# Sparse attention feeding an ELU MLP on one core: the opening and the first chunk in another order, and the second batch's masks added to its scores on TensorE

## The chip, the core and the metric

The kernel runs on one core of a Trainium2 chip. A core has five engines that each take their instructions in order: PE (TensorE, matrix multiplies, with the weight loads shown apart as PEld), DVE (VectorE), ACT (ScalarE), POOL (GpSimd) and SP (SyncE). They wait for each other through semaphores. Matrix products land in PSUM, in banks of 512 float32 columns; everything else lies in SBUF. Transfers between DRAM and SBUF are issued by POOL and SP and run on 16 DMA engines.

The metric is the device time of one execution in microseconds (us). Before the change the median of three runs is 324.32 us (323.88 to 326.67).

## The reference

Attention over 8 batches, 8 heads, 576 positions and 64 dimensions is followed by a two-layer MLP:

```python
scores = scale * np.matmul(q, k.transpose(0, 1, 3, 2))       # 8 x 8 x 576 x 576
rel = pos[:, None] - pos[None, :]
mask_local = (rel >= 0) & (rel < 32)                         # heads 0 to 3
mask_strided = (rel >= 0) & (pos[None, :] % 32 == pos[:, None] % 32)   # heads 4 to 7
scores = np.where(masks, scores, -1e9)
attn = softmax(scores)
x = (attn @ v) as 4608 tokens x 512
h = x @ w_in                                                 # 512 -> 2048
g = np.where(h > 0, h, np.exp(np.minimum(h, 0)) - 1)         # ELU
out = g @ w_out                                              # 2048 -> 512
```

A local head needs the keys of the last 32 positions; a strided head the earlier positions with the same remainder by 32, at most 18 of them. Most of the 576 x 576 scores are never computed.

## The kernel before, in words

**Attention.** A batch is worked as four pairs of heads: two strided ones (s0, s1 in batch 0, S0, S1 in batch 1) and two local ones (l0, l1). Keys and queries are brought into 126 or 108 rows (strided: seven or six residues of 18 positions) or blocks of 96 queries against 128 keys (local), so that all wanted scores lie in small blocks with a fixed mask. The steps of a pair are: `t_q` and `t_k`, transposes on PE into a PSUM bank and a copy to SBUF; `s0` and `s1`, score matmuls into the two banks of `pair_a` (L500), the exp on ACT into a probability tile `pr` (L508) and for every batch but 0 at once the mask, a multiplication of `pr` by 0 and 1 on DVE (L523; batch 0 has it as steps `m0`, `m1`); `a0` and `a1`, probabilities times values (L542), whose extra column of ones gives the sums of the softmax, then a reciprocal and a multiplication on DVE (L550, L551) into `x_s` or `x_l`; and `x`, the transposes of that (L578, L591) and the copies into `xT` (L585, L587, L595). `halo` copies 32 rows of the local values into the place where the next block of 96 reads them (L428). The strided values are loaded as `v_raw` and reordered into `v_str` by two copies (L421). From batch 3 on the transposes of q and k are made by DMAs and the steps are grouped otherwise; the change does not touch that.

**MLP.** Nine chunks of 512 tokens. `moe_in` (four matmuls of 128x512, L629) computes 128 of the 2,048 hidden units into a PSUM bank, `moe_act` takes the ELU: an exp on ACT (L655), a min and subtraction on DVE (L662), a maximum with the bank on DVE (L664). In chunk 0 the hidden blocks 4, 7, 10, 13 and 15 have a Relu on ACT (L658) and one DVE instruction (L659) in place of the last two. `moe_out` (four matmuls, L678) is one part of the second product; after four parts the result is copied by ACT (L683) and sent off by SP.

**Order.** There is no scheduler: the program order on each engine is the order in which the Python code emits. The opening (batch 0, and the first part of chunk 0) follows the list `OPENING`. In it `fill.n` are n matmuls of 128x512 whose result nobody reads, into a bank not used yet, and `moe.c` is the part of the first three blocks of chunk 0 that needs the feature group c (0 and 1 local, 2 and 3 strided) of `xT`. Then every chunk nb runs 16 steps s; batch nb + 1's attention pieces are put into gaps: gap 2s ahead of `moe_in(s)`, gap 2s + 1 behind `moe_act(s)`, then `moe_out` parts of the chunk before (for chunk 0 its own, given by `outs`). Which gap a piece takes is start + pitch x pair + offset, from `TIMES`. `ON_VECTOR` names the steps of batch 0 whose copy is made by DVE; the others are made by ACT.

**Buffers.** Scores use `pair_a` alone after the opening, so a pair's next scores wait for the exp of the last. Transposes, `av` results and `x` transposes go through a ring of three PSUM banks (`singles[:3]`): each use waits until the one three uses earlier was read. `moe_in` has the two `half` banks and, in the first part of chunk 0, `singles[3]`, which `moe_out` takes over when `share` is called at s = 10.

**Loads.** POOL issues nearly all of them. At most eight are under way: each issue waits for the one eight back. Behind the loads of batch 0 stand w_in(0), q and k and v of batch 1 with w_in(1) among them, w_in(2), w_in(3), four parts of w_out, and batch 2.

## Time and profile before

| | |
|---|---|
| median of three runs | 324.32 us (323.88 to 326.67) |
| the profiled execution | 324.63 us |
| its span, first to last instruction | 322.7 us |
| mean granted PE clock | 0.993 of full speed |
| opening, to the end of `moe.1` | 27.3 us |
| chunk 0, to the first matmul of chunk 1 | 27.3 to 55.8 us |
| last matmul | 318.2 us |

The page's second part cuts the span into 40 slices of 8.07 us; a digit is the busy share in tenths, and PEclk the clock that PE was granted. A row of the waits reads: engine, tile and line that waited, what released it, microseconds in total, times, longest. A row of the stretches gives the stretch in us, its length, then busy time and (instructions) of PE, PEld, DVE, ACT and POOL, the granted clock, the DMA share and GB/s. A row of the timeline gives start, duration, engine, line, operation, tile written<-tiles read, shapes and, in brackets, the idle time ahead of it with what ended it.

### The profile page before, as it was taken

The numbers are of one execution on the slowest core, as the hardware profiler recorded it, in microseconds if no ns is written. First come the engines' busy times: TensorE is split into PE (matmuls) and PEld (weight loads), VectorE is DVE, ScalarE is ACT, GpSimd is POOL, SyncE is SP. The second block draws the span as 40 slices with busy tenths as digits, with TensorE's granted clock in tenths as the row PEclk, the third lists the DMA queues.
The fourth block names the chain that finished last, engine by engine and source line by source line (L and its number), as shares of the span: only waits on it lengthen the run. The fifth ranks groups of instructions, "written<-read, shape, count | busy, mean of one in ns | idle before, by whom it ended". The sixth has DMA issues, their size and how long they took to land.

```text
span 322.7 us, 6076 instructions
## 1 busy us (share of the span) xinstructions
PE 304.5 (94%) x2214; PEld 151.6 (47%) x2214; DVE 244.9 (76%) x539; ACT 175.9 (55%) x334; POOL 140.1 (43%) x218
## 2 busy tenths in 40 slices
PE   1997988999999999999999999999999999999994
PEld 0564444555544544444444444444444444444443
DVE  6576887787888988989798879887988566776610
ACT  3668885776555554555555565565555534434411
POOL 9859725958957839978942840000000000000000
PEclk9999899999999999999999999999999999999999
DMA  6999999999999999999994994291110000010012
GB/s 108 159 174 121 168 207 138 145 134 174 90 149 176 141 141 186 77 159 168 196 134 102 125 208 95 71 152 58 54 51 34 35 32 35 37 62 34 35 67 72
DMA packets 108970, 36.33 MB, mean 113 GB/s; under 512 B 87357, under 2 KB 104453, under 8 KB 108933
## 3 DMA queue, kind: packets, MB, share of 16 engines
q0 software_dynamic: 71632, 18.10, 62.4%
q1 hardware_dynamic: 37301, 17.77, 26.9%
q8 instruction: 19, 0.31, 0.4%
q14 instruction: 18, 0.15, 0.1%
HBM read 36.70 MB, written 9.44 MB: 143 GB/s over the span
## 4 chain that ended last, share of the span: by engine, by line
PE 85%; DVE 6%; ACT 3%; DMA 2%; issue 1%; POOL 1%; ACTq 0%; POOLq 0%
PE single L678 37%; PE half L629 27%; PE single L629 9%; PE single L542 3%; PE pair_a L463 2%; ACT e_sb L655 2%; PE single L382 2%; DMA k_str<-in_k_dram 2%; DVE g_sb L664 1%; DVE x_l L551 1%; PE single L578 1%; DVE e_sb L662 1%; PE single L368 1%; PE pair_a L500 1%; PE single L724 1%
## 5 line engine op out<-in xcount | busy, mean ns | idle before, releaser
L678 PE MATMUL single<-w_out_sb,g_sb 128*128 128x512 bf16 (+1 forms) x592 | 145.9, 373 | 0.0
L629 PE MATMUL half<-xT,w_in_sb 128*128 128x512 bf16 x436 | 113.4, 382 | 0.0
L655 ACT ACTIVATE e_sb<-half 128x512 f32<-128x512 f32 x109 | 65.3, 599 | 69.7 <-PE half L629 67.4
L662 DVE TENSOR_SCALAR e_sb<-e_sb 128x512 bf16<-128x512 f32 x139 | 64.0, 460 | 36.0 <-ACT e_sb L655 34.9
L678 PEld LDWEIGHTS <-g_sb 128*128 128x128 bf16 x592 | 55.2, 98 | 57.6 <-DVE g_sb L664 0.2
L629 PEld LDWEIGHTS <-w_in_sb 128*128 128x128 bf16 x576 | 52.0, 98 | 56.7 <-issue 2.2
L664 DVE TENSOR_TENSOR g_sb<-e_sb,half 128x512 bf16<-128x512 bf16 x104 | 71.5, 688 | 3.7
L629 PE MATMUL single<-xT,w_in_sb 128*128 128x512 bf16 x140 | 36.5, 379 | 0.0
L655 ACT ACTIVATE e_sb<-single 128x512 f32<-128x512 f32 x35 | 21.0, 600 | 24.2 <-PE single L629 22.0
L683 ACT COPY o_sb<-single 128x512 f32<-128x512 f32 (+1 forms) x37 | 21.3, 576 | 17.0 <-PE single L678 16.7
L542 PEld LDWEIGHTS <-pr 128*128 128x128 bf16 (+3 forms) x352 | 21.0, 106 | 15.6 <-issue 0.9
L469 ACT ACTIVATE pr<-pair_a 126x936 bf16<-126x936 f32 (+1 forms) x20 | 19.2, 962 | 12.5 <-PE single L463 12.5
L180 POOL DMA_DIRECT2D k_str<-in_k_dram x32 | 20.7, 662 | 10.7 <-DMA w_in_sb<-in_moe_w_in_dram 3.0
L664 DVE TENSOR_TENSOR g_sb<-e_sb,single 128x512 bf16<-128x512 bf16 x35 | 24.1, 688 | 1.2
L180 POOL DMA_DIRECT2D v_raw<-in_v_dram x32 | 19.9, 648 | 9.4 <-DVE v_str L421 7.5
L180 POOL DMA_DIRECT2D q_str<-in_q_dram x28 | 17.6, 650 | 6.4 <-DMA w_in_sb<-in_moe_w_in_dram 1.9
L551 DVE TENSOR_TENSOR x_l<-single,rden 96x384 bf16<-96x384 f32 x32 | 17.7, 553 | 1.1
L551 DVE TENSOR_TENSOR x_s<-single,rden 126x256 bf16<-126x256 f32 (+1 forms) x32 | 15.7, 491 | 1.1
L203 POOL DMA_DIRECT2D q_loc<-in_q_dram x20 | 15.5, 817 | 2.3 <-PE single L382 0.8
L203 POOL DMA_DIRECT2D k_loc<-in_k_dram x20 | 15.8, 820 | 0.7 <-DMA q_loc<-in_q_dram 0.5
L508 ACT ACTIVATE pr<-pair_a 128x576 bf16<-128x576 f32 (+2 forms) x20 | 13.0, 652 | 5.6 <-PE pair_a L500 5.5
L550 DVE RECIPROCAL rden<-single 96x6 f32<-96x6 f32 (+2 forms) x64 | 11.9, 185 | 3.3 <-PE single L542 2.7
(114 smaller groups left out, 261.6 us busy)
## 6 DMA issues: line engine op xcount, KB each, us to landing
out_dram<-o_sb SPq DMA_DIRECT2D x35, 256.0 KB, 3.1
v_loc<-in_v_dram POOLq DMA_DIRECT2D x8, 288.0 KB, 7.9
k_str<-in_k_dram POOLq DMA_DIRECT2D x32, 67.5 KB, 5.0
v_raw<-in_v_dram POOLq DMA_DIRECT2D x32, 67.5 KB, 4.7
w_in_sb<-in_moe_w_in_dram POOLq DMA_DIRECT2D x4, 512.0 KB, 10.0
w_out_sb<-in_moe_w_out_dram POOLq DMA_DIRECT2D x4, 512.0 KB, 16.5
q_str<-in_q_dram POOLq DMA_DIRECT2D x28, 67.5 KB, 7.2
q_loc<-in_q_dram POOLq DMA_DIRECT2D x20, 64.0 KB, 4.4
```

The lines of the kernel that those rows point to most:

```text
L180: engine.dma_start(out=t[0:108, h].rearrange("p g d -> p (g d)"), in_=rows[h, :, 0:30, :].rearrange("t (r g) d -> t r (g d)", g=5))
L203: nc.gpsimd.dma_start(out=t[:, h // 2, 0:4, h % 2], in_=src[name][b, h, 0:512].rearrange("(i p) d -> p i d", p=128))
L469: nc.scalar.activation(both, sc[0:nk, :, 0:w], ACT.Exp, scale=scale)
L508: nc.scalar.activation(halves, sc[0:nk, :, 0:w], ACT.Exp, scale=scale)
L542: nc.tensor.matmul(av[0:m, p, blk - b0, :], lhsT=pr[0:nk, o:o + m], rhs=vt[0:nk, 2 * self.hp + p, blk, :], start=True, stop=True)
L551: nc.vector.tensor_tensor(self.x[0:nq, b0:b0 + n].rearrange("q g p d -> q p g d"), av[0:nq, :, 0:n, 0:D], r.unsqueeze(3).to_broadcast([nq, ...
L629: nc.tensor.matmul(hps, lhsT=w_in_sb[:, c, m * 128:(m + 1) * 128], rhs=xT[:, c, nb * N_TILE:(nb + 1) * N_TILE], start=start, stop=stop)
L655: nc.scalar.activation(e_sb, hps, ACT.Exp)
L662: nc.vector.tensor_scalar(e1_sb, e_sb, scalar1=1.0, scalar2=1.0, op0=ALU.min, op1=ALU.subtract)
L664: nc.vector.tensor_tensor(g_of[nb][:, m, :], e1_sb, hps, op=ALU.max)
L678: nc.tensor.matmul(ops, lhsT=g_of[nb][:, m, kk * 128:(kk + 1) * 128], rhs=w_out_sb[:, m, cols], start=(m == 0), stop=(m == MC - 1))
L683: nc.scalar.copy(o_sb, ops)
```

## The change

It has these parts:

1. `OPENING` puts s1.halo ahead of l1.s1, l0.a0 between s1.x and s0.x, l0.x ahead of moe.3, and S0.t_q behind moe.3; two of the eight `fill` matmuls are left out.
2. Batch 1's pieces in chunk 0 no longer come from `TIMES` but from a list `SECOND` with a gap for each. S0.t_k moves from gap 1 to 3, S0's scores from gaps 3 and 5 to 5 and 7, S1's first scores come at gap 9, the halo from gap 13 to 21 (behind `moe_act(10)`), l0.a0 from gap 19 (behind `moe_act`) to 22.
3. Batch 1's masks leave DVE. Two tiles are made in the opening, `far_s` and `far_l`, 0 where a score is wanted and -1e30 elsewhere. Ahead of the score matmuls two matmuls with the identity as weights write them into the two banks (start), and the scores are added to them (start=False); the exp then gives 0 where the mask was 0.
4. Batch 1's v_str copies go from ACT to POOL, in POOL's queue between the load of v_loc and that of w_in(3); w_in(2) is now loaded ahead of v_loc of batch 1. S1.t_q's copy goes from ACT to DVE.
5. Batch 2 starts at gap 5 of chunk 1 instead of 4. Chunk 0's three `moe_out` parts come at steps 12, 14 and 15 instead of 11, 13 and 15, and `share` is called at s = 11.

The order on PE from the end of the opening, as the two programs emit it (S0.s0+ are the far matmuls and the scores):

```
before  t_k S0 | s0 S0 | s1 S0 | moe 3 | a0 S0 | t_k S1 | moe 4 | a1 S0 | s0 S1 | moe 5 | s1 S1 | x S0 | t_q l0 | moe 6 ...
after   t_k S0 | s0+ S0 | moe 3 | s1+ S0 | t_k S1 | moe 4 | s0+ S1 | moe 5 | a0 S0 | s1+ S1 | a1 S0 | moe 6 | a0 S1 | t_q l0
        | moe 7 | a1 S1 | x S0 | t_k l0 | moe 8 | t_q l1 | x S1 | s0+ l0 | moe 9 | t_k l1 | s1+ l0 | moe 10 | s0+ l1 | a0 l0
        | moe 11 | a1 l0 | s1+ l1 | moe 12 | out | a0 l1 | x l0 | moe 13 | a1 l1 | moe 14 | out | x l1 | moe 15 | out
```

The diff, cut to its core:

```diff
 PIECES = (-2, -1, 0, 2, 3, 5, 7, 0)
 TIMES = (
     None,
-    (3, 6, (-3, -2, 0, 2, 4, 6, 9, 3)),
-    (4, 6, (-3, -2, 0, 2, 4, 6, 8, 0)),
+    None,
+    (5, 6, (-3, -2, 0, 2, 4, 6, 8, 0)),
     (2, 7, PIECES),
     ((2, 8, 15, 22), 0, PIECES),
 )
...
+SECOND = """
+3 S0.t_k 5 S0.s0 7 S0.s1 8 S1.t_k 9 S1.s0 11 S0.a0 11 S1.s1 12 S0.a1 13 S1.a0 14 l0.t_q
+15 S1.a1 15 S0.x 16 l0.t_k 17 l1.t_q 18 S1.x 18 l0.s0 19 l1.t_k 20 l0.s1 21 S1.halo 21 l1.s0
+22 l0.a0 24 l0.a1 24 l1.s1 26 l1.a0 26 l0.x 27 l1.a1 30 l1.x
+""".split()
 OPENING = """
 s0.cast_q s0.t_q s0.t_k s1.cast_q s1.t_k s0.s0 s0.m0 s1.t_q s0.s1 s0.m1 fill.2 l0.t_q s1.s1
 s1.m1 s1.s0 s1.m0 l0.t_k l1.t_q fill.1 s0.v l0.s0 l0.m0 l1.t_k l0.s1 s1.a0 s0.a0 l0.m1 l1.s0
-s1.a1 s0.a1 fill.1 l1.s1 l1.m0 fill.1 s1.halo s1.x fill.1 s0.x l1.m1 fill.1 l0.a0 fill.1 l0.a1
-l1.a0 moe.2 l1.a1 S0.t_q l0.x S1.t_q moe.3 l1.x moe.0 moe.1
+s1.a1 s0.a1 s1.halo fill.1 l1.s1 l1.m0 fill.1 s1.x l0.a0 l1.m1 fill.1 s0.x l0.a1 l1.a0 moe.2
+l1.a1 l0.x moe.3 S0.t_q l1.x S1.t_q moe.0 moe.1
 """.split()
-ON_VECTOR = "s0.t_q s1.cast_q s1.t_k l0.t_q s0.v l1.x".split()
+ON_VECTOR = "s0.t_q s1.cast_q s1.t_k l0.t_q s0.v l1.x S1.t_q".split()
 ON_SCALAR = (4, 7, 10, 13, 15)
...
     identity = consts.tile([128, 128], BF16, tag="identity")
     mask_l = consts.tile([128, S], BF16, tag="mask_l")
     mask_w = consts.tile([128, 2 * 126 + 3 * 108], BF16, tag="mask_w")
+    far_l = consts.tile([128, 3 * LB], BF16, tag="far_l")
+    far_s = consts.tile([128, 126], BF16, tag="far_s")
     mask_s, mask_s3 = mask_w[:, 0:252], mask_w[:, 252:576]
     rden = consts.tile([128, B, 2, 2, 2, 6], F32, tag="rden")
     ones = consts.tile([128, 1], BF16, tag="ones")
...
     BY_DMA = 3
     WHOLE = 3
+    FAR = 1
     raw = {}
     src = {"q": q, "k": k, "v": v}
...
     clear_v(0)
     nc.vector.memset(kT["loc"][0][:, :, 0:32], 0.0)
+    nc.vector.tensor_scalar(far_s[0:126], mask_s[0:126, 0:126], scalar1=1.0,
+                            scalar2=-NEG, op0=ALU.subtract, op1=ALU.mult)
+    nc.vector.tensor_scalar(far_l, mask_l[:, 0:3 * LB], scalar1=1.0, scalar2=-NEG,
+                            op0=ALU.subtract, op1=ALU.mult)
     load_strided(0, "k")
     load_local(0, "q")
     load_local(0, "k")
...
     load_strided(1, "v")
     load_local(1, "q")
     load_local(1, "k")
+    load_w_in(2)
     load_local(1, "v")
-    load_w_in(2)
+    for o, i in zip(rows_of(v_str[1][:, :, :, 0:D], slice(0, 4)),
+                    rows_of(raw[1], slice(0, 4))):
+        nc.gpsimd.tensor_copy(o, i)
     class Pair:
...
         def copy(self, step, late):
-            if self.b == 0:
-                late = f"{self.name}.{step}" in ON_VECTOR
+            if self.b < 2:
+                name = self.name.upper() if self.b else self.name
+                late = f"{name}.{step}" in ON_VECTOR
             return nc.vector.tensor_copy if late else nc.scalar.copy
         def cast(self, name):
...
                 return
             sc = rings["sc"].next()
             blocks = self.blocks(u)
+            far = self.b == FAR
+            if far:
+                k, n = blocks[0][4:]
+                g = len(blocks) // 2
+                if self.strided:
+                    t = far_s[0:k, 0:n].unsqueeze(1).to_broadcast([k, g, n])
+                elif u == 0:
+                    t = far_l
+                else:
+                    t = far_l[:, n:2 * n].unsqueeze(1).to_broadcast([k, g, n])
+                for bank in range(2):
+                    nc.tensor.matmul(sc[:, bank, 0:g * n], lhsT=identity[0:k, :],
+                                     rhs=t, start=True, stop=False)
             for p, blk, bank, i, nk, nq in blocks:
                 at, half = self.place(p, blk)
                 d = slice(64 * half, 64 * half + 64)
...
                 nc.tensor.matmul(sc[:, bank, i * nq:(i + 1) * nq],
                                  lhsT=kT[kind][self.b % 2][d, at, c:c + 128],
                                  rhs=qT[kind][self.b % 2][d, at, c:c + nq],
-                                 start=True, stop=True)
+                                 start=not far,
+                                 stop=not far or i == len(blocks) // 2 - 1)
             nk, nq = blocks[0][4:]
             w = len(blocks) // 2 * nq
             pr = (p_p if self.b else p_p0).tile([128, 1152 if self.b else 648], BF16, tag="pr", name="pr")
             halves = pr[0:nk, 0:2 * w].rearrange("k (a x) -> k a x", a=2)
             nc.scalar.activation(halves, sc[0:nk, :, 0:w], ACT.Exp, scale=scale)
             self.pr[u] = pr
-            if self.b:
+            if self.b and not far:
                 self.mask(u)
         def mask(self, u):
...
                         identity[0:LB, 0:LB])
                 self.copy("x", self.b > 1)(dst, xt[:, 0:S])
+    def second():
+        pairs.update((f"l{hp}", Pair(1, False, hp)) for hp in range(2))
+        gaps = {}
+        for gap, step in zip(SECOND[::2], SECOND[1::2]):
+            pair, what = step.split(".")
+            gaps.setdefault(int(gap), []).append(
+                lambda p=pairs[pair], what=what: p.step(what))
+        return gaps
     def attention(b, start, pitch, at):
         gaps = {}
         pairs = [Pair(b, s, hp) for s in (b < LATE, b >= LATE) for hp in range(2)]
...
         if b >= LATE:
             gaps[begin[0]] = [pairs[3].halo]
         for i, pr in enumerate(pairs):
-            if b == 1 and pr.strided:
-                pr.t_q = lambda: None
             for off, piece in ((at[0], pr.t_q), (at[1], pr.t_k),
                                (at[7], lambda pr=pr: pr.v_in(0)),
                                (at[7] + (b > 1), lambda pr=pr: pr.v_in(1)),
...
     def outs(nb, s):
         if nb == 0:
-            return [(0, i) for i in range(3) if s == 11 + 2 * i]
+            return [(0, i) for i in range(3) if s == (12, 14, 15)[i]]
         step = [(nb - 1, i) for i in range(3, MC)]
         if nb < n_chunks:
             step += [(nb, i) for i in range(3)]
...
     for nb in range(n_chunks + 1):
         if nb + 1 < B:
-            gaps = attention(nb + 1, *TIMES[min(nb + 1, 4)])
+            gaps = attention(nb + 1, *TIMES[min(nb + 1, 4)]) if nb else second()
             if nb == 0:
                 share([pair_a], b_halves + singles[3:], [], singles[:3])
             elif nb + 1 < LATE:
...
         if nb + 3 < B:
             load_batch(nb + 3)
         for s in range(MC):
-            if nb == 0 and s == 10:
+            if nb == 0 and s == 11:
                 share([pair_a], b_halves, singles[3:], singles[:3])
             if s == (9 if nb + 2 > LATE else 6) and nb > 0 and nb + 2 < B:
                 transpose_batch(nb + 2, int(nb + 2 >= LATE))
```

## The prediction

> **What bounds the kernel now.** I read the page first (busy shares, slices), then what TensorE (PE) waited for, then busy time and clock in short stretches, then PE's timeline against those of ScalarE (ACT) and VectorE (DVE).
>
> ```profile
> PE 304.5 (94%) x2214; PEld 151.6 (47%) x2214; DVE 244.9 (76%) x539; ACT 175.9 (55%) x334; POOL 140.1 (43%) x218
> PE   1997988999999999999999999999999999999994
> PEclk9999899999999999999999999999999999999999
> ```
>
> PE is the bound from the third slice on; only the first 56 us leave it gaps. The waits of PE name them:
>
> ```profile
> PE pair_a L500 <- ACT pr L508: 1.3, 3, 0.7
> PE single L578 <- DVE x_s L551: 1.1, 2, 0.7
> PE pair_a L500 <- ACT kT_str L371: 0.8, 1, 0.8
> PE single L542 <- ACT v_str L421: 0.5, 1, 0.5
> ```
>
> Between the opening's last fused part (end 27.31) and the first matmul of chunk 1 (55.76) the timeline shows eight waits of PE, 4.5 us together. The stretches show a second loss:
>
> ```profile
> 28.00:32.00 4.00, 2.31 (x23) 1.46 (x24) 3.81 (x7) 3.98 (x8) 4.00 (x6) 0.90 1.11 145
> 32.00:36.00 4.00, 4.00 (x29) 1.83 (x26) 3.05 (x9) 2.94 (x6) 3.88 (x7) 0.67 1.95 137
> ```
>
> DVE and ACT are full while PE is 58% busy, and then the granted clock falls: by single microseconds 0.61, 0.50, 0.50, 0.68 from 31 to 35, so 1.7 us of PE's time is lost. From 56 us to the tail the list has 0.6 us of waits left (the stretch from 100 to 200 is busy 98.9 of 100); a wait put there is a loss in full. The prize lies before 56 us: 4.5 us of waits, about 1.4 us of pipeline ends at them (a block of four lasts 1.04 but the next starts after 0.87), and 1.7 us of clock.
>
> ```profile
> 27.31 0.44 PE L368 MATMUL single<-identity,k_str 126*128 126x126 bf16 x5
> 28.52 0.28 PE L500 MATMUL pair_a<-qT_str,kT_str 64*128 64x126 bf16 x4 [0.78 <-ACT kT_str L371]
> 29.50 0.32 PE L500 MATMUL pair_a<-qT_str,kT_str 64*128 64x108 bf16 x6 [0.69 <-ACT pr L508]
> 44.79 1.04 PE L629 MATMUL half<-xT,w_in_sb 128*128 128x512 bf16 x4
> 46.98 0.69 DVE L659 SCALAR_TENSOR_TENSOR g_sb<-e_sb 128x512 bf16<-128x512 f32 x1
> 40.65 0.49 DVE L428 COPY v_loc<-v_loc 32x1280 bf16<-32x1280 bf16 x1
> ```
>
> **Added to PE.** The far matmuls stream 2x252 + 2x324 columns per strided pair and 4x288 per local pair: 1,152 each, 4,608 for four pairs, nine matmuls of 512. One costs 0.2175 us (four in 0.87), so **+1.96 us**, all on PE. Their weight loads (95 ns rows) hide as those of the score matmuls do. No accumulating row exists for such short matmuls; L629's accumulate at full rate, so I take no extra (0 to 16 x 0.1, the load row).
>
> **Taken from DVE and ACT.** Eight masks (L523, 450 ns) leave DVE: 3.6 us. The two v_str copies (0.83 + 0.63) and one qT copy (0.68) leave ACT; the qT copy costs DVE 0.47. Both engines' relief counts only where PE waits for them.
>
> **The opening.** Up to the first l1.s1 (18.68) nothing moves but two DVE instructions for the far tiles (rows 0.33 and 0.40). They delay qT's copy from 8.43 to about 9.1, before its scores at 9.87: 0 (at most 0.2). The halo copy (ACT, 1.26) goes ahead of l1.s1's exp, into ACT's 0.98 of idle time (v_loc lands at 18.1, by GpSimd's wait that ends at 18.16). So ACT reaches the two xT copies 0.8 earlier. PE follows: s1.x 19.4, l0.a0, a fill, s0.x 20.7, l0.a1 21.1, l1.a0, then moe.2 waits for s0.x's copy until 22.0 (before 22.5). x_l of l0 is done at 22.3, so l0.x stands at 22.9 (24.0) and moe.3, the q transposes, moe.0 and moe.1 follow without the waits of 0.24 and 0.28, to 25.9. The k transposes then wait for k_str, whose third piece lands at 22.32 + 3.7. They start at 26.05, not 27.31: **-1.25**.
>
> **Chunk 0**, walked by hand: each engine takes its queue in order, a block starts when its engine and inputs are free; steps on PE 0.87 (four matmuls), 0.31 or 0.24 (av), 0.23 (scores), 0.37 (12 transposes), 0.26 (5); exp 1.1 after its matmuls start, then 0.6; L662 and L664 0.46 + 0.69. The waits that remain:
> - S0.s0 at 26.55 for kT, now behind two exps: until 27.4, 0.85 (before 0.78).
> - S0.s1 has moe 3 ahead of it: 0 (0.69). S1.s0 0.22, S1.s1 0.15.
> - S0.a0 is reached at 31.6, S0.a1 at 32.5. GpSimd (POOL) ends v_loc's issue about 30.5 and then copies v_str. No such row on POOL: memsets give 0.9 ns (32x1280 in 1.16) to 1.8 ns an element (32x260 in 0.46), 1.2 to 2.3 us for 512 + 768 elements, so the ends are 31.7 to 32.8. I take 0 of wait, keep 0 to 0.3, and 0 to 0.8 for DVE (below), of which I count 0.15. Behind the copies wait w_in(3), w_out and batch 2's loads; the DMA queue is busy with earlier bytes until about 40, so their landings (w_in 42.3, w_out 45.0 to 52.7) stay, each ahead of its use here.
> - l0.t_q for S0.a0's bank 0.3; S0.x for S1.a0's bank, which DVE frees after L664 of m = 6: 0.8 (before 0.41 and 0.69 at such places).
> - moe 8 needs w_in(2), now ahead of v_loc in the queue: 35.0 (k_loc's landing) + 2.3, against 37.3: 0 to 0.3.
> - l0.s1 and l1.s0 0.2 each.
> - **l0.a0**: its third matmul reads the halo rows, whose copy now stands on DVE behind L659 of m = 10. In the rows above L659 ends 2.88 after its matmuls start (44.79 to 47.67); the copy adds 0.45. PE has 0.87 + 0.24 + 0.23 to do and then stands still: **1.75** (bounds 1.0 to 2.0).
> - l1.x for x_l behind L659 of m = 13: 0.7 (before 0.84).
>
> That is 5.2 us of waits, more than the 4.5 before. Work without waits: 16 blocks of four 13.9, scores 1.8, av 2.2, transposes 3.1, so 21, and 1.96. Chunk 0 takes 21 + 1.96 + 5.2 = 28.2 (before 55.76 - 27.31 = 28.45), its successor's first matmul comes at 54.25: only **-0.25**; what it wins (1.7 of clock, ends of pipelines), the far matmuls and the halo take. POOL against DVE: **+0.15**.
>
> **Chunk 1.** Batch 2 starts a gap later, so l0.a1 and l1.a1 stand behind moe_act on DVE. From the start of that step's matmuls: exp 1.1 to 1.7, L662 and L664 to 2.9, reciprocal and x_l to 3.6. PE reaches the fourth transpose of l0.x at 3.2 and that of l1.x at 2.95; before, x_l was done at 83.07 and 89.58, ahead of 83.53 and 89.70. New waits 0.4 and 0.7: **+1.1** (0 to 1.5).
>
> **Sum.** -1.25 - 0.25 + 0.15 + 1.1 = -0.25. The profiled execution took 324.63 (span 322.7 and 1.9 around it), 0.3 over the runs' median of 324.32. Forecast **324.4 us**.
>
> **Two rules weighed.** The trace's DVE row L662 takes 0.97 at 29.00, where POOL is issuing transfers, and 0.43 elsewhere. The Trainium skill, "SBUF — State Buffer" (§ Who interferes with whom), has VectorE and GpSimd share a port pair as an exclusive lock: a VectorE instruction with two SBUF inputs or in a two-port mode stands fully until a GpSimd instruction that reads SBUF ends. The trace agrees as far as a row can; by it L659 of m = 4 would stand for a whole copy, the sum then being 324.4 + 0.65.
> The clock: 2.0 us of waits in 27.8 to 31.2, then 3.4 us at half. The Trainium skill, "TensorE: Matmul & The Clock Gate" (Part 1), tells of a free-running window of 3.4 us whose busy share sets the next clock. The trace agrees with the length of that dip; what share decides, the page doesn't give.
>
> **Rivals.**
> - **Relief decides** (0.16): the slack on DVE and ACT is worth more than my walk grants: the halo's wait is its lower bound (-0.75), chunk 1's waits vanish (-1.1), the bank waits go (-1.1): 321.4. For it: DVE is 95% full from 28 to 32 and loses 3.6 us. Against: those waits hang on order, not on load.
> - **The clock falls behind the halo's wait, or rises late** (0.32, the slower side). From 28 to 31 PE was busy 1.6 of 3 us, and the clock fell; from 21 to 24 it was busy 2.5 of 3, and the clock stayed. Around l0.a0 it is busy about 1.6 of 3.4 us if one such stretch holds the whole wait, which is so for about half of the places where a stretch can begin; from there this rival decides. Price 1.7: 326.1. Likewise at the start: a 128x512 fill holds PE 0.39 to 0.49 until 20.8 and 0.2 from 21.3, so the full rate comes at about 21 after four fills in 3.4 us; now there are three, and a late rise costs up to 1.2: 325.6. Both: 327.3, and with POOL's 0.65 beyond 1% (0.08 of the 0.32).
> - **POOL's copies bound S0.a0 and DVE** (0.06): upper ends, 0.3 + 0.65: 325.4.
>
> **Chances.** My case 0.46 (own range 323.2 to 325.6). A measurement of this kernel tells about 1% (3.2 us) from no change: faster by that needs 321.1, most of the first rival's better half and a tail, 0.12; slower 0.10; within 0.78. The range, 321.3 to 327.0, leaves out about a tenth on either side.
>
> **What would show it.** First k_str transposes of batch 1 at 26 (opening right); PE waiting about 1.7 for DVE v_loc at l0.a0; no PE wait of 0.7 at the second strided scores; waits for DVE x_l near the end of chunk 1; a clock slice below 1 about 45 or none about 32. I am wrong if PE's waits up to 56 us sum to under 3 us, or if fill blocks are still slow after 21.

## The result: 2.1 us slower, and the profile after

Over 22 runs each, the changed kernel takes 326.04 us in the median (324.16 to 328.42) and the kernel before 323.88 (322.37 to 326.67): the ratio is 1.0066, 95% interval 1.0046 to 1.0085, or 2.1 us (1.5 to 2.8). The profiled execution of the changed kernel took 325.94, its span 323.5. The difference is small but clear of the scatter of the runs.

Not all of it lies between the first and the last instruction. Each run has its time and its span on record: over the 22 runs of the change the time outside the span is 2.74 us in the median (2.36 to 3.28). Over the 92 runs of the kernel before that stand beside the variants below it is 1.84 (1.75 to 1.96), and its median span is 321.9 to 322.3 against 323.25 for the change. So about 0.9 us of the 2.1 are lost outside the span, where every run of the change lies above all of those 92, and about 1.0 to 1.3 inside it. What is done outside the span no trace here shows.

In the lines of the changed kernel, `moe_in` is L669, its exp L695, `moe_act` on DVE L702 and L704 (with ACT's Relu: L698 and L699), `moe_out` L718, the far matmuls L525, the scores L533, `av` L576, x on DVE L585, its transposes L612 and L625, the halo's copy L448.

From the page of the changed kernel, the busy times and the rows of 40 slices of 8.09 us (busy tenths of PE, granted clock):

```profile
PE 298.3 (92%) x2187; PEld 149.9 (46%) x2228; DVE 241.5 (75%) x534; ACT 172.9 (53%) x331; POOL 139.9 (43%) x220
PE   1788679999999999999999999999999999999994
PEclk9999999999999999999999999999999999999999
```

DVE and ACT are lighter by 3.4 and 3.0 us, as the change meant, and the dip of the clock between 31 and 35 us is gone. PE is nevertheless emptier in slices 5 and 6 (32 to 49 us; slices 2 and 3 lie in the opening, with two fills fewer and a wait of 1.07 us for kT_loc), and its list of waits says for what (line that waited, what released it, us in total, times, longest):

```profile
PE single L625 <- DVE x_l L585: 2.3, 4, 0.6
PE single L576 <- DVE v_loc L448: 1.8, 1, 1.8
...
PE single L669 <- DMA w_in_sb<-in_moe_w_in_dram: 1.1, 1, 1.1
PE single L612 <- DVE x_s L585: 1.0, 2, 0.7
```

PE's timeline has them in order of time (start, duration, instruction, and in brackets the idle time ahead with what ended it):

```profile
25.79 0.43 PE L388 MATMUL single<-identity,k_str 126*128 126x126 bf16 x5 [0.54 <-DMA k_str<-in_k_dram]
...
38.43 1.04 PE L669 MATMUL single<-xT,w_in_sb 128*128 128x512 bf16 x4 [1.11 <-DMA w_in_sb<-in_moe_w_in_dram]
...
46.07 0.30 PE L576 MATMUL single<-v_loc,pr 128*128 128x65 bf16 x4 [1.78 <-DVE v_loc L448]
...
85.04 0.30 PE L625 MATMUL single<-identity,x_l 96*128 96x96 bf16 x3 [0.54 <-DVE x_l L585]
...
92.00 0.30 PE L625 MATMUL single<-identity,x_l 96*128 96x96 bf16 x3 [0.61 <-DVE x_l L585]
```

The first row is where the opening ends. Each of the four waits behind it stands at a place that the change moved. Two are in chunk 0: block 8 needs w_in(2), and l0.a0 needs the halo rows. The other two, the transposes of l0 and l1 of batch 2 in chunk 1, had no row in the profile before. DVE's timeline shows why the halo is late: its copy stands behind the L699 of hidden block 10, which itself waited for ACT's Relu.

```profile
44.80 0.69 DVE L699 SCALAR_TENSOR_TENSOR g_sb<-e_sb 128x512 bf16<-128x512 f32 x1 [1.27 <-ACT e_sb L698]
45.52 0.49 DVE L448 COPY v_loc<-v_loc 32x1280 bf16<-32x1280 bf16 x1
```

Stage by stage, in the two profiled executions:

| stretch, us | before | after | difference |
|---|---|---|---|
| to the first k_str transposes of batch 1 | 27.31 | 25.79 | -1.5 |
| from there to the first matmul of chunk 1 | 28.45 | 29.79 | +1.3 |
| chunk 1 | 35.93 | 37.42 | +1.5 |
| chunk 2 to the end of the span | 231.0 | 230.5 | -0.5 |
| span | 322.7 | 323.5 | +0.8 |

The runs differ by more than these two spans, since the profiled execution before was 0.75 us over the median of its runs and that after 0.1 under, and since the time outside the span grew.

The first row of the table compares more than two orders. In every execution PE's rows are slow at first and go to full rate at some moment, while the granted clock of the stretches reads 1.00 in that slow part already. In the profiled execution before, that moment came at 21 us, in that of the change at 13, as the same twelve transposes show (before, then after):

```profile
13.39 0.69 PE L382 MATMUL single<-identity,k_loc 96*64 96x96 bf16 x12
13.47 0.45 PE L402 MATMUL single<-identity,k_loc 96*64 96x96 bf16 x12
```

Run e8_far_alone below has the opening of the kernel before and full rate from 13.5 us, and it comes to the first k_str transposes as early as the change does:

```profile
25.94 0.44 PE L385 MATMUL single<-identity,k_str 126*128 126x126 bf16 x5
```

So the -1.5 of that row is not the worth of the new opening, and what chunk 0 loses behind it belongs in part to this early execution. The section on the opening takes this up.

### The profile page after: what moved, and what is told of

It is laid out like the page before. It is cut to its first block, busy times and chain, and to the rows that moved or that the text cites. A ratio compares the mean times of both kernels' runs of the same rounds, so it can differ in the third digit from the quotient of the medians.

```text
span 323.5 us, 6059 instructions
## 1 busy us (share of the span) xinstructions
PE 298.3 (92%) x2187; PEld 149.9 (46%) x2228; DVE 241.5 (75%) x534; ACT 172.9 (53%) x331; POOL 139.9 (43%) x220
## 4 chain that ended last, share of the span: by engine, by line
PE 78%; DMA 8%; DVE 5%; POOL 3%; ACT 2%; issue 2%; ACTq 0%; POOLq 0%
PE single L718 36%; PE half L669 25%; PE single L669 9%; DMA w_in_sb<-in_moe_w_in_dram 3%; PE single L576 3%; DMA q_str<-in_q_dram 2%; DMA k_loc<-in_k_dram 2%; PE pair_a L483 2%; DVE g_sb L704 1%; DVE e_sb L702 1%; POOL k_str L191 1%; ACT e_sb L695 1%; PE single L612 1%; DVE x_l L585 1%; POOL v_raw L191 1%
## 5 line engine op out<-in xcount | busy, mean ns | idle before, releaser
L718 PE MATMUL single<-w_out_sb,g_sb 128*128 128x512 bf16 (+1 forms) x571 | 142.7, 373 | 1.6 <-issue 0.8
L669 PE MATMUL half<-xT,w_in_sb 128*128 128x512 bf16 x424 | 110.8, 379 | 1.3 <-issue 0.5
L695 ACT ACTIVATE e_sb<-half 128x512 f32<-128x512 f32 x109 | 65.2, 599 | 75.0 <-PE half L669 71.0
L702 DVE TENSOR_SCALAR e_sb<-e_sb 128x512 bf16<-128x512 f32 x139 | 62.3, 448 | 39.4 <-ACT e_sb L695 38.8
L718 PEld LDWEIGHTS <-g_sb 128*128 128x128 bf16 x592 | 54.6, 98 | 56.0
L669 PEld LDWEIGHTS <-w_in_sb 128*128 128x128 bf16 x576 | 52.7, 98 | 58.4 <-DMA w_in_sb<-in_moe_w_in_dram 1.2
L704 DVE TENSOR_TENSOR g_sb<-e_sb,half 128x512 bf16<-128x512 bf16 x104 | 71.5, 688 | 3.6
L669 PE MATMUL single<-xT,w_in_sb 128*128 128x512 bf16 x134 | 35.7, 379 | 1.4 <-DMA w_in_sb<-in_moe_w_in_dram 1.1
L695 ACT ACTIVATE e_sb<-single 128x512 f32<-128x512 f32 x35 | 21.0, 600 | 25.4 <-PE single L669 22.9
L576 PEld LDWEIGHTS <-pr 128*128 128x128 bf16 (+3 forms) x352 | 20.2, 102 | 15.7 <-issue 2.2
L489 ACT ACTIVATE pr<-pair_a 126x936 bf16<-126x936 f32 (+1 forms) x20 | 19.2, 962 | 12.5 <-PE single L483 12.5
L704 DVE TENSOR_TENSOR g_sb<-e_sb,single 128x512 bf16<-128x512 bf16 x35 | 24.1, 688 | 1.2
L191 POOL DMA_DIRECT2D k_str<-in_k_dram x32 | 19.9, 645 | 9.1 <-issue 3.0
L191 POOL DMA_DIRECT2D q_str<-in_q_dram x28 | 18.7, 726 | 6.3 <-DMA w_out_sb<-in_moe_w_out_dram 2.0
L585 DVE TENSOR_TENSOR x_l<-single,rden 96x384 bf16<-96x384 f32 x32 | 17.7, 554 | 1.2
L585 DVE TENSOR_TENSOR x_s<-single,rden 126x256 bf16<-126x256 f32 (+1 forms) x32 | 15.7, 491 | 1.1
L214 POOL DMA_DIRECT2D q_loc<-in_q_dram x20 | 15.5, 798 | 1.0 <-DMA k_str<-in_k_dram 0.6
```

The source lines that it names most:

```text
L191: engine.dma_start(out=t[0:108, h].rearrange("p g d -> p (g d)"), in_=rows[h, :, 0:30, :].rearrange("t (r g) d -> t r (g d)", g=5))
L214: nc.gpsimd.dma_start(out=t[:, h // 2, 0:4, h % 2], in_=src[name][b, h, 0:512].rearrange("(i p) d -> p i d", p=128))
L489: nc.scalar.activation(both, sc[0:nk, :, 0:w], ACT.Exp, scale=scale)
L576: nc.tensor.matmul(av[0:m, p, blk - b0, :], lhsT=pr[0:nk, o:o + m], rhs=vt[0:nk, 2 * self.hp + p, blk, :], start=True, stop=True)
L585: nc.vector.tensor_tensor(self.x[0:nq, b0:b0 + n].rearrange("q g p d -> q p g d"), av[0:nq, :, 0:n, 0:D], r.unsqueeze(3).to_broadcast([nq, ...
L669: nc.tensor.matmul(hps, lhsT=w_in_sb[:, c, m * 128:(m + 1) * 128], rhs=xT[:, c, nb * N_TILE:(nb + 1) * N_TILE], start=start, stop=stop)
```

## The experiments

All times are medians; ratios are to the kernel before, run on the same chip, with a 95% interval. Differences between two variants are differences of their ratios, their uncertainty the root of the two intervals' squares.

| run | what it is | us | ratio to before |
|---|---|---|---|
| (the change) | | 326.04 | 1.0066 (1.0046 to 1.0085) |
| e1_halo | the change, halo a gap earlier | 323.49 | 0.9979 (0.9954 to 1.0005) |
| e2_start4 | the change, batch 2 from gap 4 | 325.22 | 1.0024 (0.9992 to 1.0055) |
| e3_v_first | the change, w_in(2) behind v_loc | 329.62 | 1.0158 (1.0111 to 1.0204) |
| e4_masks_dve | the change, masks on DVE | 327.99 | 1.0104 (1.0071 to 1.0137) |
| e5_halo_start4 | e1 and e2 together | 323.55 | 0.9984 (0.9953 to 1.0015) |
| e6_opening_alone | before with the new opening | 324.42 | 1.0005 (0.9972 to 1.0037) |
| e7_w_in_earlier | e5 with w_in(2) ahead of k_loc | 322.92 | 0.9963 (0.9928 to 0.9997) |
| e8_far_alone | before with the far matmuls | 324.51 | 1.0021 (0.9988 to 1.0055) |
| e9_copies_act | the change, v_str copies on ACT | 327.58 (326.87 without the longest) | 1.0116 (1.0089 to 1.0143) |
| e10_again | e7 once more | 323.06 | 0.9977 (0.9956 to 0.9999) |
| e11_w_out_later | e7 with w_out's last part later | 322.95 | 0.9975 (0.9958 to 0.9992) |
| e12_old_opening | e7 with the opening of before | 324.18 | 1.0025 (1.0004 to 1.0046) |

### The halo's place

```diff
-20 l0.s1 21 S1.halo 21 l1.s0
+20 l0.s1 20 S1.halo 21 l1.s0
```

The copy is emitted ahead of the block's ELU instead of behind it.

> The changed kernel with batch 1's halo copy put into gap 20 instead of 21, so that it stands ahead of the last ELU instruction of block 10 on VectorE. Theory 'order' (the changed kernel is slower through three waits that its order makes: halo 1.8 us, the two x_l waits in chunk 1 1.15 us, w_in(2) 1.1 us): the halo wait of TensorE (1.78) falls under 0.4 and the time by 1.3 to 1.8 us, 0.4 to 0.55% of the changed kernel. Theory 'far matmuls' (the 1.96 us of mask matmuls on TensorE are the loss and the waits only show where slack lies): the time stays within 0.4 us, as the wait turns up elsewhere. Theory 'clock' (a stretch at half rate follows the halo wait in some executions): the fall is up to 3 us, and fewer executions show a mean clock of 0.992.

Measured: 323.49 us, 2.8 us (1.0 either way) less than the change. The wait for v_loc is gone; in the stretch of three microseconds that held it (stretch, length, then busy us and instructions of PE, PEld, DVE, ACT, POOL, then granted clock, DMA share, GB/s) PE is now full:

```profile
43.00:46.00 3.00, 3.00 (x36) 1.56 (x34) 2.15 (x6) 2.73 (x6) 0.84 (x2) 1.00 1.25 208
```

In the changed kernel that row reads

```profile
43.00:46.00 3.00, 1.29 (x13) 0.58 (x12) 1.70 (x3) 2.06 (x4) 0.74 (x2) 1.00 1.23 202
46.00:49.00 3.00, 2.77 (x27) 1.55 (x28) 1.83 (x6) 1.33 (x3) 0.40 (x1) 1.00 1.24 207
```

One line of a list, one place earlier, is the largest single loss of the change that a run shows. It is worth more than the 1.78 us of idle time that the trace shows, though only at the edge of the uncertainty. Two things may make up the rest. The time outside the span is 0.3 us shorter (2.45 against 2.74). And the mean granted clock differs: with the halo late, 8 of 22 runs have 0.991 to 0.993 and take 326.6 us in the mean, the other 14 take 325.5; with it early, none of 12 is below 0.996.

### Batch 2's start

```diff
-    (5, 6, (-3, -2, 0, 2, 4, 6, 8, 0)),
+    (4, 6, (-3, -2, 0, 2, 4, 6, 8, 0)),
```

> The changed kernel with batch 2 starting at gap 4 of chunk 1 again. Theory 'order': the waits for x_l before the fourth transpose of l0.x and l1.x in chunk 1 (0.54 and 0.61) vanish and the time falls by 1.0 to 1.5 us. Theory 'far matmuls': no change beyond 0.4 us. A third possibility: batch 2's q and k land too late for the earlier start, TensorE waits for k_str at its first key transposes, and the time stays or rises.

Measured: 325.22 us, 1.4 us (1.2 either way) less than the change. Both waits for x_l in chunk 1 are gone, and chunk 1 is back at 35.93 us in the trace. This execution also shows what the clock can do behind the halo's wait, which is the same in it:

```profile
43.00:46.00 3.00, 1.22 (x17) 0.64 (x16) 1.44 (x3) 1.79 (x4) 1.03 (x2) 1.00 1.23 203
46.00:49.00 3.00, 2.98 (x21) 1.30 (x19) 1.26 (x4) 0.60 (x1) 0.09 (x1) 0.50 1.24 206
```

With 1.22 of 3 us busy PE is at half clock for the next three microseconds; with 1.29 the changed kernel's profiled execution stayed at full clock. The same hole cost the clock in one execution and not in the other. The Trainium skill, "TensorE: Matmul & The Clock Gate" (Part 1), explains such a difference by a window of 3.4 us that runs free of the kernel; the two rows agree with that, and do not show it. On the same page ("Why this matters for your kernels") the Trainium skill advises to keep gaps of PE under some 3 us; here a gap of 1.8 us, with a busy share of 41% around it, was enough in one execution.

### Where w_in(2) stands in the queue

```diff
-    load_w_in(2)
     load_local(1, "v")
+    load_w_in(2)
```

> The changed kernel with w_in(2) loaded behind v_loc of batch 1 again. If w_in(2)'s landing is what holds the ninth hidden block (wait 1.11 in the changed kernel), it lands about 2.5 us later, TensorE waits some 3 to 3.6 us there, and the time rises by 1.5 to 2.5 us, less what the earlier v_loc gives. If that wait is cover for another, the time stays within 0.4 us.

Measured: 329.62 us, 3.0 us (1.6 either way) more than the change. PE's wait at block 8 is twice as long, and the clock falls behind it (waits, then the stretches):

```profile
PE single L669 <- DMA w_in_sb<-in_moe_w_in_dram: 2.4, 1, 2.4
```

```profile
37.00:40.00 3.00, 0.79 (x17) 0.56 (x16) 1.37 (x4) 1.61 (x4) 2.70 (x3) 0.88 1.25 205
40.00:43.00 3.00, 2.76 (x20) 1.25 (x21) 0.14 (x1) 0.77 (x2) 1.35 (x3) 0.50 1.24 208
43.00:46.00 3.00, 2.67 (x17) 1.00 (x18) 0.97 (x2) 1.74 (x4) 1.02 (x2) 0.50 1.25 210
```

1.3 us more of waiting cost 3.0 us of time: the half clock lasts from 39.3 to 46.1. The move of w_in(2) ahead of v_loc was thus needed in the new order. It was not enough for the profiled execution of the change, where PE came early; in the profiles of e1 and e2, which keep the move, PE came 0.8 to 1.1 us later and the wait is 0.16 or nothing.

### The masks, in the new order and in the old

```diff
-    FAR = 1
+    FAR = -1
```

With that the masks of batch 1 go back to DVE in the changed kernel.

> The changed kernel in its new order, but batch 1's masks multiplied by VectorE as before. Theory 'far matmuls': TensorE gets 1.96 us back and the time falls by 1 to 2 us. Theory 'order': VectorE gets 8 x 0.45 = 3.6 us more between 26 and 50 us, where it has waits of its own, and each av waits for its mask; the time stays within 0.7 us or rises.

Measured: 327.99 us, 1.2 us (1.2 either way) more than the change. PE saves the far matmuls and waits instead:

```profile
PE single L576 <- DVE pr L557: 1.2, 1, 1.2
```

```profile
31.00:34.00 3.00, 1.71 (x22) 0.98 (x19) 2.97 (x5) 2.38 (x5) 3.00 (x5) 1.00 1.24 180
34.00:37.00 3.00, 1.86 (x26) 1.28 (x24) 2.90 (x9) 0.60 (x1) 2.88 (x7) 0.89 1.71 175
37.00:40.00 3.00, 2.43 (x17) 1.41 (x15) 2.52 (x5) 1.62 (x3) 2.70 (x3) 0.50 1.86 164
```

DVE is full from 31 to 37, PE is 60% busy, and the clock goes to half. All 12 runs have a mean clock of 0.983 to 0.993.

The other way round, the far matmuls in before's order:

```diff
+            far = self.b == FAR
...
+                for bank in range(2):
+                    nc.tensor.matmul(sc[:, bank, 0:g * n], lhsT=identity[0:k, :],
+                                     rhs=t, start=True, stop=False)
...
-            if self.b:
+            if self.b and not far:
                 self.mask(u)
```

This is the kernel before with the change's third part alone: its own `OPENING`, `TIMES`, loads, v_str copies and `moe_out` steps are kept.

> The kernel before, everything in its old order, with batch 1's masks added by TensorE alone. TensorE gets 1.96 us of matmuls, VectorE loses 3.6 us of masks. If TensorE's time is what counts in chunk 0: ratio 1.004 to 1.006. If VectorE's queue is what the av and transposes wait for there: the waits for x_s and x_l and the dip of the clock about 31 us shrink by as much or more, ratio 0.996 to 1.002. In the changed order the masks on VectorE cost 0.6% more than on TensorE, which speaks for the second.

Measured: 324.51 us, ratio 1.0021 (0.9988 to 1.0055): no difference. In this order too PE pays for the matmuls, but none of the 12 runs has a clock below 0.994, against 24 of 92 runs of the kernel before. The median span is that of the kernel before (322.05 against 322.2); what the medians of the times differ by lies outside the span (2.55 against 1.84), which suggests that the loss there comes with the far matmuls or with the two tiles made for them (with the tiles, but the masks on DVE, it is 2.17 in e4). So the far matmuls seem to trade PE time for a clock that stays up, and come out even in the old order, and about 1 us ahead of the masks on DVE in the new one. This profiled execution, too, came early to block 8 and stood 1.20 us for w_in(2); the far matmuls in the old order with that load earlier were not tried.

### Both order mends, and w_in(2) earlier

> The changed kernel with both order faults mended: the halo copy in gap 20 and batch 2 starting at gap 4 of chunk 1. If the two losses are separate, their gains add: the halo alone gave a ratio to the kernel before of 0.998, the start alone 0.4% under the changed kernel, so 0.993 to 0.995, a time of 321.7 to 322.5 us. If batch 2's q and k hold the earlier start once chunk 0 is shorter (TensorE then waits for k_str or q_str of batch 2 about 55 us), the ratio stays at 0.998.

The edit is that of e1 and that of e2. Measured: 323.55 us, the same as the halo's mend alone (323.49). The two gains do not add. What is late next stands on DVE (DVE's timeline, then PE's):

```profile
58.00 0.69 DVE L704 TENSOR_TENSOR g_sb<-e_sb,half 128x512 bf16<-128x512 bf16 x1
61.03 0.85 DVE L441 COPY v_str<-v_raw 126x512 bf16<-126x512 bf16 x1 [2.34 <-DMA v_raw<-in_v_dram]
```

```profile
63.32 1.02 PE L669 MATMUL half<-xT,w_in_sb 128*128 128x512 bf16 x4 [0.46 <-DVE g_sb L704]
```

DVE stands 2.34 us for batch 2's strided values, its ELU waits behind, and PE for that. GpSimd can issue that load only when earlier ones have landed: its own timeline in this run puts the five v_raw issues at 54.6 to 57.6 us, behind waits for w_out. Across the profiled executions the effect looks like a floor:

| run | first matmul of chunk 1 | DVE's wait for v_raw | first matmul of chunk 2 | chunk 1 |
|---|---|---|---|---|
| e7_w_in_earlier | 52.8 | 2.33 | 90.5 | 37.6 |
| e5_halo_start4 | 53.6 | 2.34 | 90.4 | 36.8 |
| e10_again | 54.6 | 1.81 | 90.9 | 36.3 |
| e12_old_opening | 54.9 | 0.29 | 90.8 | 35.9 |
| e8_far_alone | 55.1 | 0.96 | 91.0 | 35.9 |
| e2_start4 | 56.9 | 0 | 92.8 | 35.9 |

Whoever enters chunk 1 before about 54.9 us leaves it at 90.4 to 90.9 all the same. Not all of that is the 0.3 to 0.5 us that PE waits for g_sb; e7 also has 0.35 for k_str of batch 2 and 0.34 for a mask behind the v_raw copy.

The next variant, in addition, loads w_in(2) earlier:

```diff
-    load_local(1, "k")
     load_w_in(2)
+    load_local(1, "k")
```

> The kernel with the halo copy in gap 20 and batch 2 at gap 4, and w_in(2) loaded ahead of k_loc of batch 1 as well. If w_in(2)'s landing still holds block 9 in it, the wait for DMA w_in_sb goes, one for k_loc of 0 to 0.7 us may come at l0.t_k, and the time is 0.3 to 1.0 us under that of the kernel without this edit. If no execution was held there, the two are within 0.3 us, or this one is slower by the wait for k_loc.

Measured: 322.92 us, 0.9963 (0.9928 to 0.9997), and once more over 12 other runs:

> The kernel with S1.halo at gap 20, batch 2 from gap 4 and w_in(2) ahead of k_loc once more, over more runs. If its 0.9963 was real: 0.993 to 0.999 of the time before, 322.9 us; if it was the luck of twelve runs: 1.000.

323.06 us, 0.9977 (0.9956 to 0.9999). No wait for w_in(2) is left in either, but e5's trace had none either, since PE came there later; against e5 the gain is 0.7 us and not certain (1.5 either way). The change with these three mends is some 0.7 to 1.2 us faster than the kernel before, and 3 us faster than the change itself. It is the best found here, and both intervals end just under 1. Against the kernel before it gains 1.4 to 1.7 us of span and gives back 0.55 to 0.6 outside.

### The opening

> The kernel before with the new order of the opening alone (two fills fewer, halo copy earlier). By the prediction's step the first k transposes of batch 1 come 1.25 us earlier and nothing takes that back: ratio 0.996. Rival: w_in(2), which lands at the moment the kernel before needs it (TensorE reaches the ninth hidden block at 40.06, the landing is seen by GpSimd at 40.1), takes all of it: TensorE waits 0.8 to 1.3 us for DMA w_in_sb at that block and the ratio is 0.999 to 1.001. Rival of the clock: fewer fills, late full rate, ratio above 1.002.

Only `OPENING` is exchanged in the kernel before (and `ON_VECTOR` left as it was). Measured: 324.42 us, 1.0005 (0.9972 to 1.0037): nothing. Its list of waits has one at the hidden block that needs w_in(2) (L629 is `moe_in` there):

```profile
PE single L629 <- DMA w_in_sb<-in_moe_w_in_dram: 0.9, 1, 0.9
```

But this execution is no example of a gain that the load takes. PE reaches that block at 41.2 us, later than before (40.06). The granted clock was 0.50 from 18.6 to 25.5 us, behind waits of 0.71 for v_str and 0.32 for x_s, and the first k_str transposes come only at 28.23. Seven of the 12 runs have a clock below 0.994 (324.8 us in the mean; the other five 323.4). So this run leaves open whether the load or the clock took the gain, or whether there was none. Where w_in(2) comes early enough, the opening can be taken away instead, from e7:

```diff
-s1.a1 s0.a1 s1.halo fill.1 l1.s1 l1.m0 fill.1 s1.x l0.a0 l1.m1 fill.1 s0.x l0.a1 l1.a0 moe.2
-l1.a1 l0.x moe.3 S0.t_q l1.x S1.t_q moe.0 moe.1
+s1.a1 s0.a1 fill.1 l1.s1 l1.m0 fill.1 s1.halo s1.x fill.1 s0.x l1.m1 fill.1 l0.a0 fill.1 l0.a1
+l1.a0 moe.2 l1.a1 S0.t_q l0.x S1.t_q moe.3 l1.x moe.0 moe.1
```

> As e10_again with the opening in before's order. If the new opening is worth the 1.25 us that I forecast, and only w_in(2) and the clock hid it: 1.2 us slower than e10_again (324.1), with S0's first k_str transposes 1 us or more later on average. If the new opening brings nothing (its eight profiles so far start S0's k transposes at 25.8 to 28.2 us, the old opening's two at 25.9 and 27.3): within 0.6 us of e10_again.

Measured: 324.18 us against 323.06 beside it: 1.1 us by the medians, 1.6 (1.0 either way) by the ratios. That is near the forecast's 1.25, but half of the 1.1 lies outside the span, which the forecast's step does not touch: 3.01 us against 2.45. The median spans differ by 0.6 (321.1 against 320.5), which twelve runs each hardly tell from nothing.

Single profiles settle it only where PE's rows go to full rate at about the same moment:

| opening | profiled execution | PE at full rate from about | first k_str transposes of batch 1 |
|---|---|---|---|
| new | the change, e7 | 13, 12.5 | 25.79, 25.98 |
| new | e3, e5, e4, e2 | 22 to 22.5 | 26.29, 26.43, 26.50, 26.61 |
| new | e1 | 21.5 | 27.13 |
| new | e9, e10, e11 | 23.5, 24.5, 26.5 | 27.30, 27.77, 28.99 |
| new | e6 | 15.5 to 18.6, again from 25.5 | 28.23 |
| old | e8 | 13.5 | 25.94 |
| old | before | 21 | 27.31 |
| old | e12 | 22.5 | 27.80 |

With full rate from about 13 us both orders come out at 25.8 to 26.0, and the new one then stands 0.5 for the load of k_str. With full rate from 22 to 22.5 the new one is 1.2 to 1.5 ahead of the one old execution there is. At 21 us PE is still slow in nine of the eleven profiles with the new opening and in one of the three with the old. So the gain depends on a moment that differs from one execution to the next by more than the gain itself, and the forecast's 1.25 is neither shown nor refuted.

### The v_str copies

```diff
-3 S0.t_k 5 S0.s0 7 S0.s1
+3 S0.t_k 5 S0.s0 6 S0.v 7 S0.s1
...
-    for o, i in zip(rows_of(v_str[1][:, :, :, 0:D], slice(0, 4)),
-                    rows_of(raw[1], slice(0, 4))):
-        nc.gpsimd.tensor_copy(o, i)
```

> The changed kernel with batch 1's two v_str copies on ScalarE again (issued at gap 6 of chunk 0, behind the first strided scores) and none on GpSimd. My reading (GpSimd's copies cost VectorE 0.63 us once, at the L699 of 1.32 us, which PE does not feel): no gain, 0 to 0.8 us slower than the changed kernel (326.0 to 326.8), since ScalarE takes back 0.83 + 0.63 us where its exps feed PE; the stretched L699 at about 31 us is 0.69 again, and a PE wait of 0.3 to 0.8 for ScalarE v_str or for pr appears. Rival (GpSimd's copies and the port they hold are part of the loss): 0.6 us or more faster than the changed kernel, 325.4 or less.

Measured: 327.58 us over six runs, 326.87 without the longest (331.66), which is the profiled one; the ratio, too, leaves it out and gives 1.6 us (1.1 either way) more than the change. From that profile only the order is read. ACT's timeline:

```profile
29.17 0.60 ACT L539 ACTIVATE pr<-pair_a 126x504 bf16<-126x504 f32 x1
31.24 1.36 ACT L438 COPY v_str<-v_raw 126x512 bf16<-126x512 bf16 x2 [1.47 <-DMA v_raw<-in_v_dram]
```

ACT stood 1.47 us for the transfer, with two exps behind it that PE needed. On POOL the same wait (0.27) stops nobody. So the run is a measurement of this place in ACT's order as well as of the copy itself; what the copies would cost on ACT later in its order was not tried. Taking the copies off POOL in this way gains nothing; how little they cost there is read from their rows, in the account below.

### w_out's last part later

```diff
-    for i in range(4):
+    for i in range(3):
+        load_w_out(i)
...
-    load_batch(2)
+    load_strided(2, "q")
+    load_w_out(3)
+    load_strided(2, "k")
+    load_strided(2, "v")
+    for name in "qkv":
+        load_local(2, name)
```

> As the kernel beside it (halo at 20, batch 2 from 4, w_in(2) first), with the fourth piece of w_out issued behind batch 2's q_str instead of ahead of it. My reading (after these mends PE runs ahead of GpSimd's DMA queue: batch 2's v_raw lands at 61 us whatever PE does, VectorE stands 2.3 us for it, and PE 0.46 us for g_sb behind that): the issue of v_raw comes about 1 us earlier, VectorE's wait is 1.3 us or less, PE's wait for g_sb at 63 us shrinks or goes, 0.3 to 0.6 us faster. Rival (the bytes ahead in the queue bind, not GpSimd's issuing): v_raw lands when it did, the time is the same within 0.2 us, or slower if w_out's piece is now late for the first output part of chunk 1 at 54 us.

Measured: 322.95 us against 323.06: no difference. The first v_raw issue comes 1.3 us earlier (53.8 against 55.1), the last 0.6, and DVE's wait is gone:

```profile
61.86 0.69 DVE L704 TENSOR_TENSOR g_sb<-e_sb,half 128x512 bf16<-128x512 bf16 x1
62.47 0.35 DVE L441 COPY v_str<-v_raw 126x512 bf16<-126x512 bf16 x1
```

But this execution entered chunk 1 only at 56.6 us, where e2 had no such wait either. So the wait's absence here proves little, the time speaks for neither side, and what makes up the floor of chunk 1 stays open: v_raw is one part of it, the loads of batch 2 ahead of it may be another.

## Why the prediction was right, and where it was wrong

The forecast of no measurable change (324.4 us, within 1%) held in kind: 326.04 is 0.66% slower and inside the range of 321.3 to 327.0. In size it was 1.6 us off, and the result lies outside the range that the prediction gave its own case (323.2 to 325.6). By its own steps:

- **The opening** (-1.25). -1.5 in the trace, on the mark by luck: in that execution PE's rows are at full rate from 13 us, in the one before from 21, and the old opening with full rate from 13.5 (e8) is as early. The step fits executions whose rate rises at about 22 us (1.2 to 1.5 ahead of the one old execution there is); for a rise at 13 the prediction had no term. Timed, the opening brings nothing alone (e6) and 0.6 us of span with w_in(2) out of the way (e12 against e10).
- **The halo behind L659** (1.75 of wait). 1.78, on the instruction that the prediction named. Right. But the prediction booked it inside a chunk 0 that came out 0.25 faster, so that the largest loss of the change stood in the text as one of nine waits. Taking it away gives 2.8 (1.0 either way).
- **w_in(2) at block 8** (0 to 0.3). 1.1: **the step that failed in kind.** PE came there at 37.3 us, as the prediction had it, but the transfer landed at 38.4. The landing was worked out by adding 2.3 us to that of k_loc from the old profile; it is also later in e1 (38.6). In this execution PE's early start was paid straight into this wait. In e1, e2 and e5, where PE came at 38.1 to 38.5, it is 0.16 or nothing, so not every run of the change need have it.
- **The other waits of chunk 0** (5.2 with the halo). They sum to 5.26 in the trace, by luck: w_in(2) is 1.1 too many, while kT (0.56 for 0.85), both S1 scores (none for 0.37) and both local scores (none for 0.4) are about as much too few.
- **The far matmuls** (1.96). From start to start the rows give 2.7, as in these of PE's timeline, where two far matmuls stand 0.37 and 0.35 us ahead of the scores:

```profile
28.09 0.44 PE L525 MATMUL pair_a<-far_s,identity 108*128 108x324 bf16 x2
28.46 0.32 PE L533 MATMUL pair_a<-qT_str,kT_str 64*128 64x108 bf16 x6
...
47.26 0.41 PE L525 MATMUL pair_a<-far_l,identity 128*128 128x288 bf16 x2
47.61 0.30 PE L533 MATMUL pair_a<-qT_loc,kT_loc 64*128 64x96 bf16 x6
```

  The eight pairs take 0.31, 0.37, 0.31, 0.37 and four times 0.34 to 0.35 (the first, ahead of a wait, taken as its like). Columns alone gave 0.21 to 0.28 for each; the bound "0 to 16 x 0.1" held, at 16 x 0.05. **Mis-sized by 0.8.**
- **Work without waits** (21). 29.79 less 5.26 less 2.74 is 21.8: **mis-sized by 0.8.** The prediction named the ends of pipelines at waits (1.4 before) and then dropped them from the sum whole, as if the new order had no waits, while its own list had 5.2 us of them. That these ends are the 0.8 is likely; no run shows it.
- **Chunk 1** (+1.1: 0.4 and 0.7). +1.5 in the trace, 0.54 and 0.61 at the two places named; 1.4 by the run that takes them away. The mechanism is right, the size 0.4 too small.
- **POOL against DVE** (+0.15, and by the port rule 0.65). The copies took 1.39 us, inside the bounds, and held one DVE instruction, as the two timelines of the changed kernel show (POOL, then DVE):

```profile
30.57 1.39 POOL L353 COPY v_str<-v_raw 126x512 bf16<-126x512 bf16 x2 [0.27 <-DMA v_raw<-in_v_dram]
```

```profile
31.18 1.32 DVE L699 SCALAR_TENSOR_TENSOR g_sb<-e_sb 128x512 bf16<-128x512 f32 x1 [0.96 <-ACT e_sb L698]
```

  L699 takes 0.69 elsewhere, so 0.63 is lost there. This is what the Trainium skill, "SBUF — State Buffer" (§ Who interferes with whom), says of an instruction with two SBUF inputs beside a GpSimd instruction that reads SBUF, and the trace agrees. DVE runs without a pause from there to the x_s that PE's next wait is for (0.53, at the q_loc transposes); where no copy holds L699, that wait is 0.21 (e1, e2, e10) or 0.53 as well (e5), and in e7, where L699 took 1.01, it is 0.22. So by these rows PE lost at most 0.3 by it, and the 0.15 was a fair size.
- **The clock rival** (326.1, chance in the 0.32 of the slower side). Its figure is the result's, by luck: it is not the whole cause. The profiled execution of the changed kernel lost no clock and still took 325.94. The mechanism is real: half clock behind the halo in e2, 8 of 22 runs below 0.994 and 1.2 us longer. Over all runs that is about 0.4 us, and the kernel before has such runs too (24 of 92). Its second half, a late rise at the start, is met in most profiles with the new opening, though not in that of the change.
- **Relief decides** (321.4). DVE was relieved, and what that brought did not exceed the price of the far matmuls: e8 is at 1.0021.
- **The time outside the span** (kept at 1.9). 2.74 in the median of the runs: **a term that the prediction took as fixed without a reason**, and 0.9 of the 2.1 us. It is 1.81 with the new opening alone (e6), 2.17 with the masks on DVE (e4) and 2.55 with the far matmuls alone (e8); the cause stays open.

What the sum came to: in the profiles -1.5 + 1.3 + 1.5 - 0.5 = +0.8 of span, for a forecast of -0.25; the rest of the 2.1 us is that the forecast stood on a profiled execution 0.75 us over the runs' median, that the one after was 0.1 under its own, and that the time outside the span was 2.4 us after and 1.9 before. Its first two terms, -1.5 and +1.3, depend on when PE's rate rose and say little one by one.

## What to carry to other kernels

An earlier start is worth nothing past the next transfer: before a gain in one stage is booked, look up when the loads that the next stages need land, and move those loads with it (here w_in(2), then batch 2's values). In an order written by hand a step's place behind or ahead of a neighbour on the same engine can outweigh everything the change is about: one copy placed a gap too late cost 2.8 us, and moving eight masks from that engine to PE won 1.2 in the new order and nothing in the old. A wait of PE can cost more than its length where the busy share around it is near a half (1.3 us more of wait cost 3.0 in e3), so that work which fills PE may pay for itself in the clock. Before the stages of two profiled executions are set side by side, compare rows of the same shape in both: where PE went to full rate at different moments, the stages differ by more than the change does. And a kernel's span is not its time: here 0.9 us of the loss lay outside it.

## What the runs showed of the hardware that was not expected

- The clock fell to half behind single waits of 1.8 us (e2) and 2.4 us (e3), for 3.4 and 6.8 us. A hole of the same size (1.22 and 1.29 us busy of 3) cost it in one execution and not in another.
- PE's rows are slow from the start (twelve transposes 0.69 us, later 0.45), and the moment of full rate came anywhere from 12.5 to 26.5 us in fourteen profiled executions. In that first slow part the granted clock of the stretches reads 1.00 all the same.
- The time outside the span was 1.75 to 1.96 us in 92 runs of the kernel before and 2.36 to 3.28 in 22 runs of the change.
- Two matmuls with the identity ahead of accumulating score matmuls take 0.31 to 0.37 us for 252 to 324 columns each, 0.05 us apiece more than the rate of the 512-column rows gives.
- POOL copies 512 and 768 bf16 elements a partition in 1.39 to 1.66 us together (ten profiles), while DVE takes 0.35 and 0.36 for the same two (e11, e5) when nothing holds it. The first took 1.65 at 60.4 us in e12, beside six memsets of POOL (60.3 to 61.9).
